# A gated recurrence and its feed-forward layer: the last stores behind the branch, the verdict in the fifth block, a unit between a block's first pieces

## The chip, the cores and the metric

One core of one Trainium2 chip runs the kernel. The metric is the device time of one execution in microseconds (us). The kernel before takes 513.67 us, the median of 3 runs (513.63 to 514.79). TensorE is called PE here, VectorE DVE, ScalarE ACT, GpSimd POOL and SyncE SP; SP issues most of the DMAs.

## The reference

The input of the feed-forward layer is the output of a gated recurrence over 768 steps, 4 batches, 8 heads and 48 channels:

```python
f = 1.0 / (1.0 + np.exp(-f_logit))
for t in range(S):                                   # S = 768
    state = f[:, :, t, :, None] * state + np.einsum('bhd,bhe->bhde', k[:, :, t], v[:, :, t])
    y[:, :, t] = np.einsum('bhd,bhde->bhe', q[:, :, t], state)
x = y.transpose(0, 2, 1, 3).reshape(B * S, H * D)    # 3072 x 384
h = x @ w_in                                         # 384 -> 2048
r = np.maximum(h, 0.0)
return (r * r) @ w_out                               # 2048 -> 384
```

All of it is float32.

## The kernel before

*Blocks and pieces.* The 768 steps are cut into 6 blocks (`NBLK`) of 128 steps; with 4 batches a block has 512 columns. The feed-forward layer of a block is 16 pieces `f` (`NF`) of 128 hidden channels. Each float32 operand is held as a high and a low part, and a product is three matmuls. For each piece `up(f)` is nine matmuls of 128x512 into one hidden bank of PSUM (`ph`, line 246); `square(f)` is three ACT instructions (relu L256, square L257, cast to `gh` L258); `rest(f)` is one DVE instruction (`gl`, L263), the last reader of the bank; `down(f)` is nine matmuls (L272) into the three output banks `po`. `run` issues `up(n)`, `square(n)`, `rest(n)` and then `down(n - 2)` (`LAG`). So at a block's start up(0), up(1) and up(2) follow each other on PE with no down between them, and later up and down alternate. There are two hidden banks, `ps_h0` and `ps_h1`, which take turns (`bank`).

*Order.* Block 0's first 6 pieces are issued from a table written by hand, together with the decoding of the first weights. Then `order` runs block 1 whole, the other 10 pieces of block 0, and blocks 2 to 5 whole. PE, DVE, ACT and SP keep program order.

*Units.* The recurrence is split into units, four per block (three of their own loads and a fourth put together from what the three leave over). A unit's stages, by their letters: L and v loads (DMAs on SP), G gates (ACT), K keys (DVE, POOL), Q queries (DVE), m a copy of the last keys and queries (DMA on SP), T four transposes into the PSUM tile `pk` (PE, L460), N copies out of it (`kn`, ACT, L466), D state sums and S scores, both into `ds` (PE, L484 and L495), r, M, C the crossed rows, the mask and the chain of states (ACT, DVE), s a copy of the states (`sx`, ACT, L454), Y outputs into `py` (PE, L538 and L550), H, X, g and h parts that write the next block's `x`. `hook(k, n, place, do)` puts a stage at run k behind or ahead of piece n: place 0 is ahead of `up(n)`, 0.5 behind `square(n)`, 0.7 behind `rest(n)`, 1 behind `down(n - 2)`. A tuple (n, place, stages) in `STAGE_AT` is relative to the unit's own piece, which is in `UNIT_AT` (`THIRD_AT` for block 2, which is built during blocks 1 and 0); `OUT_AT` is the piece of the outputs. During block b the units of block b + 1 are built. All of a unit's PSUM tiles (`pk`, `ds`, `py` and the like) come from the pool `ps_a`.

*Decoding.* The weights come in as packed words; the 20 halves that remain for block 0's second part are decoded during block 1 on ACT (L139, cast L171) and DVE (L153 to L160, L173), some three halves per two pieces.

*The end.* `finish` copies the three output banks of the last block on ACT, DVE and ACT and issues its stores on SP. Then a verdict is found: the least value in `low` and a test of `sums` (DVE, L853 to L861) go through a PE transpose (`pl`, L863) into a `flag`, all engines read it (`values_load`, L868), and the branch `tc.If(rv > 0)` (L869) leads around a general path, which handles inputs that the fast path cannot. It isn't entered with these inputs. L928 is the closing of the program.

Of the kernel before, what the change touches and what calls it, by code (L numbers as in the profile page):

```python
# [12 lines left out]
F32 = mybir.dt.float32  # L13
# [65 lines left out]
class Moe:  # L79


    def __init__(self, ctx, tc, const, sums, out):
        self.tc, self.nc, self.sums, self.out = tc, tc.nc, sums, out

        self.const, self.raw, self.w, self.ps, self.turns = const, {}, {}, {}, 0
        self.xs, self.spares, self.w4 = [], 0, None

        self.floor = const.tile([P, 1], F32, name="floor")
        tc.nc.vector.memset(self.floor, -31.0 / 64.0)
# [135 lines left out]
        ]  # L225

    def bank(self, f):
        self.ph[f] = self.ps["ps_h1" if self.turns % 2 else "ps_h0"].tile(
            [P, 512], F32, tag="ph", name=f"ph{self.blk}_{f}"
        )  # L230
        self.turns += 1

    def up(self, f, last=True):
# [30 lines left out]
            out=gl, in0=self.ph.pop(f), in1=gh.bitcast(F32), op=ALU.subtract  # L264
        )

    def down(self, f):
        gh, gl = self.g.pop(f)
        for e in range(NJ):
            wh, wl = (self.w[f, 1][:, i, e * P : (e + 1) * P] for i in range(2))  # L270
            for i, (l, r) in enumerate(((wh, gl), (wl, gh), (wh, gh))):
                self.nc.tensor.matmul(  # L272
                    self.po[e], lhsT=l, rhs=r, start=f == self.fs[0] and i == 0,
                    stop=f == self.fs[-1] and i == 2,
                )
# [49 lines left out]
def fast_path(ctx, tc, moe, ident, low, fkqT, vN, w, w4, out):  # L325
    nc = tc.nc
# [344 lines left out]
    with tc.manual_schedule(engines={ET.PE, ET.SP, ET.DVE, ET.Activation}):  # L671
        with tc.tile_pool(name="ps_p", bufs=2, space=bass.MemoryType.PSUM) as ps_p:
            for t in FIRST.split():
                step(t)
        moe.psum(ctx, "ps_h1", "ps_o")

        moe.sums_of()
        for t in SECOND.split():
            step(t)
        part = moe.keep()  # L680
        whole = half[0] + half[1]
        order = [(1, whole), (0, half[1])] + [(blk, whole) for blk in range(2, NBLK)]
# [14 lines left out]
        halves = [(f, i) for f in half[1] for i in range(2)]  # L697
        steps = [moe.decode(f, i, pro, False) for f, i in halves]
        for n in range(NF - 1):
            few = range(3 * n // 2, min(3 * (n + 1) // 2, len(halves)))  # L700
            for h in few:
                if n < AHEAD:
                    weights_load(*halves[h])
                else:
                    hook(0, n - AHEAD, 0.5, lambda h=h: weights_load(*halves[h], mark=True))

            def before(few=few):
                for h, last in zip(few, (None, *few)):
# [12 lines left out]

            hook(0, n, 0, before)
            hook(0, n, 0.5, after)
            hook(0, n, 0.7, last)
        hook(0, NF - 1, 0, third)
        for blk in range(2, NBLK):
            first = 0 if blk == 2 else (blk - 1) * NF - LO
            ats = (THIRD_AT, THIRD_OUT_AT) if blk == 2 else (UNIT_AT, OUT_AT)
            for j, (at, out_at) in enumerate(zip(*ats)):
                un = Unit(blk * HP + j, xs, (ps_a,))  # L730
                for n, place, stage in STAGE_AT if un.own else LAST_AT:
                    hook(0, first + at + n, place, lambda un=un, stage=stage: un.stage(stage))
                out_stage = "YHX" if un.own else "YHXhg"
                hook(0, first + out_at, 1, lambda un=un, stage=out_stage: un.stage(stage))
        for k, (blk, fs) in enumerate(order):
            if blk > 1 and blk + 1 < NBLK:
                xs[blk + 1] = moe.new_x(blk + 1, (0, 1, 2)[blk - 2])
            moe.start(blk, xs[blk], fs)
            moe.run(hooks[k])
            moe.finish(lambda e: out[blk, e * P : (e + 1) * P], None if blk else part)  # L740


def general_path(ctx, tc, moe, ident, fkqT, vN, w, out):

    nc = tc.nc
    dram = ctx.enter_context(tc.tile_pool(name="dram", bufs=1, space=bass.MemoryType.DRAM))
    xs = dram.tile([HP, D, 2, B, S], F32, name="xs")
    with ExitStack() as att:
        pool = att.enter_context(tc.tile_pool(name="gen", bufs=1))
# [6 lines left out]
        for hp in range(HP):  # L756
# [16 lines left out]
            ff = src["f"]  # L773
# [67 lines left out]
@with_exitstack  # L841
def tile_kernel(ctx: ExitStack, tc: tile.TileContext, fkqT, vN, w, w4, out):
    nc = tc.nc
    const = ctx.enter_context(tc.tile_pool(name="const", bufs=1))
    ident = const.tile([P, P], F32, name="ident")
    low = const.tile([P, NBLK * NJ, B * NC], F32, name="low")
    sums = const.tile([P, 2 * NF], F32, name="sums")
    moe = Moe(ctx, tc, const, sums, out)
    with ExitStack() as fast:
        fast_path(fast, tc, moe, ident, low, fkqT, vN, w, w4, out)  # L850


    flag = const.tile([1, 1], I32, name="flag")  # L853
    with tc.tile_pool(name="ps_l", bufs=1, space=bass.MemoryType.PSUM) as ps_l:
        good = const.tile([P, 2], F32, name="good")
        nc.vector.tensor_reduce(
            out=good[:, 0:1], in_=low.rearrange("p u n -> p (u n)"), axis=mybir.AxisListType.X, op=ALU.min
        )
        nc.vector.tensor_scalar(out=sums, in0=sums, scalar1=MOST, scalar2=None, op0=ALU.is_lt)
        nc.vector.tensor_reduce(out=good[:, 1:2], in_=sums, axis=mybir.AxisListType.X, op=ALU.min)  # L860
        nc.vector.tensor_tensor(out=good[:, 0:1], in0=good[:, 0:1], in1=good[:, 1:2], op=ALU.min)  # L861
        pl = ps_l.tile([1, P], F32, name="pl")
        nc.tensor.transpose(out=pl, in_=good[:, 0:1], identity=ident)  # L863
        least = const.tile([1, 1], F32, name="least")
        nc.vector.tensor_reduce(out=least, in_=pl, axis=mybir.AxisListType.X, op=ALU.min)
        nc.vector.tensor_scalar(out=least, in0=least, scalar1=LOWEST, scalar2=None, op0=ALU.is_le)
        nc.vector.tensor_copy(out=flag, in_=least)
    rv = nc.values_load(flag[0:1, 0:1], min_val=0, max_val=1)  # L868
    with tc.If(rv > 0):  # L869
# [63 lines left out]
```

## Time and profile before

| | |
|---|---|
| median of 3 runs | 513.67 us (513.63 to 514.79) |
| the profiled execution | 515.19 us, its span 513.4 us |
| TensorE clock granted, mean | 0.996 |
| PE busy | 490.2 us, 95% of the span |
| PEld (weight loads) busy | 390.0 us, 76% |
| ACT busy | 285.1 us, 56% |
| DVE busy | 261.4 us, 51% |
| POOL busy | 29.2 us, 6% |

A profile's page shows one execution. Its span runs from the first to the last recorded instruction. In the rows of the timeline the columns are the start, the duration, the engine, the line of the kernel, the operation, output and inputs, a shape and a count; brackets at the end give the idle time just before and whose work ended it. In the rows by line, the part ahead of the bar names the operation, its shape and count; behind it stand the busy time in us and the mean in ns of one instruction, then the idle time before it. The waits are sum, count and median. SPq, DVEq and ACTq are the sequencers of these engines; their rows of a line give the minimum, median and maximum duration in ns and the first and last time of it.

### The profile page before, as it was taken

The page shows a single profiled execution, that of the slowest core. Times are in us where ns is not written, and L with a number is a line of the kernel's source. Part 1 is how long each engine was busy: PE and PEld are TensorE (multiplying, and loading weights), DVE is VectorE, ACT ScalarE, POOL GpSimd, SP SyncE. Part 2 cuts the span into 40 slices and gives each one's busy share as a digit, 9 for nine tenths or more (in the row PEclk, how much of TensorE's full clock was granted, in tenths as well). Part 3 has the DMA queues.
Part 4 walks back from the last instruction along what each step waited for, and adds up shares of the span by engine and source line. Part 5 has one row for each costly group of instructions (what it writes and reads, how often), then busy time and mean ns, then how long its engine had stood idle before and what let it go on. Part 6 is the DMA issues. An engine that isn't in the chain of part 4 may idle for free.

```text
span 513.4 us, 11450 instructions
## 1 busy us (share of the span) xinstructions
PE 490.2 (95%) x4831; PEld 390.0 (76%) x4831; DVE 261.4 (51%) x479; ACT 285.1 (56%) x579; POOL 29.2 (6%) x66
## 2 busy tenths in 40 slices
PE   6689899999999999999999999999999999999994
PEld 5577676888777778778787787787777787788883
DVE  7899977988847263554353445353346222211111
ACT  4689748877756563554544555454555543544441
POOL 6112010001000000000000000000000000000000
PEclk9999999999999999999999999999999999999998
DMA  8982026473332116203005313004410001100001
GB/s 284 312 301 68 13 69 244 133 250 107 88 90 48 42 22 172 77 15 88 3 5 145 109 28 89 1 1 119 139 28 12 1 1 32 62 1 1 0 1 68
DMA packets 20364, 41.97 MB, mean 82 GB/s; under 512 B 2656, under 2 KB 5728, under 8 KB 20304
## 3 DMA queue, kind: packets, MB, share of 16 engines
q1 hardware_dynamic: 19856, 40.23, 25.9%
q0 software_dynamic: 448, 0.92, 0.8%
q8 instruction: 40, 0.66, 0.5%
q14 instruction: 20, 0.16, 0.1%
HBM read 31.69 MB, written 4.72 MB: 71 GB/s over the span
## 4 chain that ended last, share of the span: by engine, by line
PE 82%; DVE 9%; ACT 3%; DMA 3%; issue 1%; SPq 0%; POOL 0%; DVEq 0%; ACTq 0%
PE po L272 37%; PE ph L246 35%; PE ds L495 2%; PE ds L484 2%; PE py L538 2%; DMA last_kq<-fkq 2%; PE py L550 2%; DVE fkq L410 1%; PE pk L460 1%; DMA fkq<-in_fkqT_dram 1%; DVE gl L263 1%; DVE fkq L424 1%; ACT gh L258 1%; ACT ph L257 1%; ACT ph L256 1%
## 5 line engine op out<-in xcount | busy, mean ns | idle before, releaser
L246 PE MATMUL ph<-x,w 128*128 128x512 f32 x864 | 221.8, 402 | 3.1 <-DVE gl L263 3.1
L246 PEld LDWEIGHTS ph<-x,w 128*128 128x128 f32 x864 | 159.8, 189 | 43.2 <-DVE gl L263 5.8
L272 PE MATMUL po<-gh,w 128*128 128x512 f32 x576 | 181.0, 395 | 0.3 <-DVE w L173 0.3
L263 DVE TENSOR_TENSOR gl<-ph,gh 128x512 fp32r<-128x512 f32 x96 | 66.2, 690 | 186.7 <-ACT gh L258 186.6
L256 ACT ACTIVATE ph<-ph 128x512 f32<-128x512 f32 x96 | 55.9, 582 | 142.2 <-PE ph L246 142.2
L272 PEld LDWEIGHTS po<-gh,w 128*128 128x128 f32 x576 | 107.9, 187 | 26.8 <-DVE w L173 0.6
L272 PE MATMUL po<-gl,w 128*128 128x512 f32 x288 | 114.1, 396 | 0.0
L272 PEld LDWEIGHTS po<-gl,w 128*128 128x128 f32 x288 | 54.0, 187 | 13.3 <-issue 0.2
L258 ACT CAST gh<-ph 128x512 fp32r<-128x512 f32 x96 | 56.3, 586 | 3.0
L257 ACT ACTIVATE ph<-ph 128x512 f32<-128x512 f32 x96 | 55.9, 582 | 3.0
L415 POOL TENSOR_SCALAR fkq<-fkq 128x8 f32<-128x8 f32 x18 | 11.8, 657 | 326.1 <-DVE fkq L410 308.6
L410 DVE TENSOR_TENSOR_SCAN fkq<-fz,dr 128x520 f32<-128x520 f32 x18 | 22.2, 1235 | 4.8 <-ACT fz L405 4.8
L538 PEld LDWEIGHTS py<-sc,vn 64*64 64x64 f32 (+1 forms) x640 | 17.9, 126 | 8.1 <-issue 7.0
L171 ACT CAST w<-wa 128x384 fp32r<-128x384 f32 (+1 forms) x33 | 16.8, 510 | 12.4 <-DVE wa L160 10.5
L424 DVE TENSOR_TENSOR_SCAN fkq<-fz,dz 128x520 f32<-128x520 f32 x18 | 22.3, 1241 | 0.6
L538 PE MATMUL py<-sc,vn 64*64 64x64 f32 (+1 forms) x640 | 21.1, 222 | 0.7 <-DVE sc L502 0.7
L502 DVE TENSOR_TENSOR sc<-ds,mask 128x512 f32<-128x512 f32 x24 | 16.5, 689 | 10.2 <-PE ds L495 9.6
L139 ACT ACTIVATE wa<-raw 128x384 f32<-128x384 f32 (+1 forms) x33 | 18.1, 550 | 5.1 <-DMA raw<-in_w_dram 5.0
L550 PE MATMUL py<-rx,sx 48*48 48x64 f32 (+1 forms) x320 | 20.3, 217 | 0.1
L460 PE MATMUL pk<-ident,fkq 128*128 128x128 f32 x72 | 13.6, 318 | 5.3 <-DVE fkq L416 3.4
L156 DVE SCALAR_TENSOR_TENSOR wa<-raw,wa 128x384 int32<-128x384 int32 (+1 forms) x33 | 18.1, 552 | 0.8
L454 ACT COPY sx<-sp 48x208 f32<-48x208 f32 x44 | 16.0, 365 | 3.9 <-DVE sp L517 2.9
(92 smaller groups left out, 408.2 us busy)
## 6 DMA issues: line engine op xcount, KB each, us to landing
fkq<-in_fkqT_dram SPq DMA_DIRECT2D x17, 768.0 KB, 5.6
raw<-in_w_dram SPq DMA_DIRECT2D x32, 384.0 KB, 5.3
vn<-in_vN_dram SPq DMA_DIRECT2D x24, 192.0 KB, 5.1
out_dram<-ob SPq DMA_DIRECT2D x15, 256.0 KB, 2.3
x<-ys SPq DMA_DIRECT2D x30, 64.0 KB, 2.4
last_kq<-fkq SPq DMA_DIRECT2D x28, 64.5 KB, 2.3
out_dram<-part SPq DMA_DIRECT2D x3, 256.0 KB, 2.1
last_kq<-fkq POOLq DMA_DIRECT2D x8, 64.5 KB, 5.8
```

The costliest lines, as they stand in the source:

```text
L139: nc.scalar.activation(a, upper_f, AF.Abs, scale=2.0**-112, **kw)
L246: self.nc.tensor.matmul(self.ph[f], lhsT=w[:, i], rhs=x[:, j], start=first and n == 0, stop=last and n == 2)
L256: nc.scalar.activation(ph, ph, AF.Relu)
L257: nc.scalar.activation(ph, ph, AF.Square)
L258: nc.scalar.copy(out=gh, in_=ph)
L263: self.nc.vector.tensor_tensor(out=gl, in0=self.ph.pop(f), in1=gh.bitcast(F32), op=ALU.subtract)
L272: self.nc.tensor.matmul(self.po[e], lhsT=l, rhs=r, start=f == self.fs[0] and i == 0, stop=f == self.fs[-1] and i == 2,)
L410: V.tensor_tensor_scan(out=rr[:, ::-1], data0=self.fz[:, NZ * CZ : 0 : -1], data1=dr[:, ::-1], initial=0.0, op0=ALU.mult, op1=ALU.add,)
L424: V.tensor_tensor_scan(out=pp, data0=self.fz[:, : NZ * CZ], data1=dz, initial=0.0, op0=ALU.mult, op1=ALU.add)
L460: nc.tensor.transpose(out=self.pk[:, b], in_=self.kt[:, b * TB : (b + 1) * TB], identity=ident)
L538: nc.tensor.matmul(self.py[h * C : h * C + m, c, b * C : (b + 1) * C], lhsT=self.vn[rows, b, h * D : h * D + m], rhs=self.sc[rows, h, b], ...
L550: nc.tensor.matmul(self.py[h * C : h * C + m, c, b * C : (b + 1) * C], lhsT=s[rows, b * D : b * D + m], rhs=q[rows], start=False, stop=b = ...
```

## The change

Five things are changed.

1. One unit per block gets stages of its own, `EARLY_AT`: its transposes stand behind up(0) of the run (`UNIT_AT` 0 in place of −3), its state sums behind up(1). That is unit 0 of blocks 3, 4 and 5; of block 2, which is built around block 0's second part, it is unit 1, with its own piece at 16 in place of 15.
2. The decoding of the remaining weights stands one piece later in block 1; the first part stands whole behind `rest(1)`.
3. The verdict is found in block 4 (the fifth), behind `down(10)` of piece 12, and read by the engines in block 5 behind piece 12. Its transpose uses the tile `pk` of `ps_a`; the pool of its own is gone.
4. In block 5, for which no unit is built any more, the hidden banks rotate over three: `ps_h0`, `ps_h1` and `pk`. Its last two downs are interleaved by output bank, and all three copies are DVE's.
5. The last block's stores stand behind the branch in SP's program. The general path now writes its outputs of the last block and loads them back into the copied tiles first.

The diff, without the lines that only move the verdict's instructions:

```diff
+EARLY_AT = ((-4, 0, "Lv"), (-2, 1, "GK"), (-1, 0.5, "Q"), (-1, 1, "m"), (0, 1, "TN"), (1, 1, "DSrMC"), (2, 1, "s"))
-UNIT_AT, OUT_AT = (-3, 3, 6, 9), (3, 6, 9, 13)
-THIRD_AT, THIRD_OUT_AT = (11, 15, 18, 21), (15, 18, 21, 23)
+UNIT_AT, OUT_AT = (0, 3, 6, 9), (3, 6, 9, 13)
+THIRD_AT, THIRD_OUT_AT = (11, 16, 18, 21), (15, 18, 21, 23)
+EARLY, THIRD_EARLY = 0, 1
+VERDICT_AT = 12
...
     def bank(self, f):
+        n = self.turns % (3 if self.third_bank else 2)
+        pool, tag = (self.ps[f"ps_h{n}"], "ph") if n < 2 else (self.third_bank, "pk")
+        self.ph[f] = pool.tile([P, 512], F32, tag=tag, name=f"ph{self.blk}_{f}")
...
-    def run(self, hooks):
+    def run(self, hooks, obs=None):
         for n in range(len(self.fs) + LAG):
+            if obs and n == len(self.fs):
+                for e in range(NJ):
+                    for f in self.fs[-LAG:]:
+                        self.down(f, (e,))
+                    self.nc.vector.tensor_copy(out=obs[e], in_=self.po[e])
+                return
...
-        for n in range(NF - 1):
-            few = range(3 * n // 2, min(3 * (n + 1) // 2, len(halves)))
+        for n in range(1, NF - 1):
+            few = range(3 * (n - 1) // 2, min(3 * n // 2, len(halves)))
...
-            hook(0, n, 0, before)
-            hook(0, n, 0.5, after)
-            hook(0, n, 0.7, last)
+            for place, do in zip((0, 0.5, 0.7) if n > 1 else (0.7, 0.7, 0.7), (before, after, last)):
+                hook(0, n, place, do)
...
-                for n, place, stage in STAGE_AT if un.own else LAST_AT:
+                for n, place, stage in EARLY_AT if j == early_unit else STAGE_AT if un.own else LAST_AT:
...
+        hook(len(order) - 2, VERDICT_AT, 1, lambda: general.append(verdict(nc, moe, low, ident, ps_a)))
+        hook(
+            len(order) - 1, VERDICT_AT, 1,
+            lambda: general.append(nc.values_load(general[0][0:1, 0:1], min_val=0, max_val=1)),
+        )
...
-            moe.run(hooks[k])
-            moe.finish(lambda e: out[blk, e * P : (e + 1) * P], None if blk else part)
+            if blk == NBLK - 1:
+                moe.third_bank = ps_a
+                obs = [moe.gp.tile([P, NT], F32, tag=f"part{e}", name=f"ob_last{e}", bufs=1) for e in range(NJ)]
+                moe.run(hooks[k], obs)
+                moe.third_bank = None
+            else:
+                moe.run(hooks[k])
+                moe.finish(lambda e: out[blk, e * P : (e + 1) * P], None if blk else part)
+    return general[1], obs
...
     with tc.If(rv > 0):
         with ExitStack() as gen:
             general_path(gen, tc, moe, ident, fkqT, vN, w, out)
+        for e in range(NJ):
+            nc.sync.dma_start(obs[e], out[NBLK - 1, e * P : (e + 1) * P])
+    for e in range(NJ):
+        nc.sync.dma_start(out[NBLK - 1, e * P : (e + 1) * P], obs[e])
```

In the rows that follow the numbers after a name are block, then unit or piece, then a running number; the lines of the changed kernel stand some lines lower (up is L251 there, down L277, the transposes L472, the state sums L496, the scores L507, the verdict's transpose L781, the branch L899).

PE at the start of block 3, before; `w15_1` is the last down of block 2, `w0_0` the first up of block 3:

```order
L272 MATMUL po2_0_2_2544<-gh2_15_3301,w15_1_1791 128x512 x2
L246 MATMUL ph3_0_3351<-x3_0_2539,w0_0_524 128x512 x3
L246 MATMUL ph3_0_3351<-x3_1_2540,w0_0_524 128x512 x3
L246 MATMUL ph3_0_3351<-x3_2_2541,w0_0_524 128x512 x3
L246 MATMUL ph3_1_3367<-x3_0_2539,w1_0_486 128x512 x3
L246 MATMUL ph3_1_3367<-x3_1_2540,w1_0_486 128x512 x3
L246 MATMUL ph3_1_3367<-x3_2_2541,w1_0_486 128x512 x3
L246 MATMUL ph3_2_3387<-x3_0_2539,w2_0_731 128x512 x3
```

The same place of PE after, where `pk4_0` and `ds4_0` belong to unit 0 of block 4:

```order
L277 MATMUL po2_0_2_2494<-gh2_15_3248,w15_1_1824 128x512 x2
L251 MATMUL ph3_0_3301<-x3_0_2489,w0_0_524 128x512 x3
L251 MATMUL ph3_0_3301<-x3_1_2490,w0_0_524 128x512 x3
L251 MATMUL ph3_0_3301<-x3_2_2491,w0_0_524 128x512 x3
L472 MATMUL pk4_0_3317<-ident_58,fkq4_0_3108 128x128 x4
L251 MATMUL ph3_1_3325<-x3_0_2489,w1_0_486 128x512 x3
L251 MATMUL ph3_1_3325<-x3_1_2490,w1_0_486 128x512 x3
L251 MATMUL ph3_1_3325<-x3_2_2491,w1_0_486 128x512 x3
L496 MATMUL ds4_0_3341<-vn4_0_3110,kn4_0_3322 64x48
...
L507 MATMUL ds4_0_3341<-fkq4_0_3108 64x64 x16
L251 MATMUL ph3_2_3387<-x3_0_2489,w2_0_731 128x512 x3
```

The transposes moved in between up(0) and up(1), the state sums and scores (32 small matmuls, most of them in the rows left out) between up(1) and up(2); before, they stood in block 2's pieces 13 and 14.

DVE at piece 12 of block 4, after; before, the `gl` of pieces 12 and 13 were neighbours:

```order
L268 TENSOR_TENSOR gl4_12_4731<-ph4_12_4720,gh4_12_4730 128x512
L774 TENSOR_REDUCE good_4746<-low_59 128x1
L777 TENSOR_SCALAR sums_60<-sums_60 128x32
L778 TENSOR_REDUCE good_4746<-sums_60 128x1
L779 TENSOR_TENSOR good_4746<-good_4746 128x1
L783 TENSOR_REDUCE least_4753<-pl_4751 1x1
L784 TENSOR_SCALAR least_4753<-least_4753 1x1
L785 CAST flag_4745<-least_4753 1x1
L268 TENSOR_TENSOR gl4_13_4768<-ph4_13_4757,gh4_13_4767 128x512
```

Between these two `gl` the verdict's seven instructions now stand; the fifth of them waits for PE's transpose. On PE after, at the same place:

```order
L277 MATMUL po4_0_2_4106<-gl4_10_4637,w10_1_1487 128x512
L277 MATMUL po4_0_2_4106<-gh4_10_4636,w10_1_1487 128x512 x2
L781 MATMUL pl_4751<-ident_58,good_4746 1x128
L251 MATMUL ph4_13_4757<-x4_0_3295,w13_0_1614 128x512 x3
L251 MATMUL ph4_13_4757<-x4_1_3296,w13_0_1614 128x512 x3
```

The transpose of `good` moved in between down(10) and up(13). SP's end before:

```order
L868 TENSOR_LOAD flag_5310
L868 ISA x2
L314 DMA out_0_dram<-ob4_0_4878 128x512
L314 DMA out_0_dram<-ob4_1_4881 128x512
L314 DMA out_0_dram<-ob4_2_4884 128x512
L314 DMA out_0_dram<-ob5_0_5290 128x512
L314 DMA out_0_dram<-ob5_1_5293 128x512
L314 DMA out_0_dram<-ob5_2_5296 128x512
L869 COMPARE_AND_BRANCH
```

and after, where the rows left out are those of the general path:

```order
L326 DMA out_0_dram<-ob4_2_4898 128x512
L752 TENSOR_LOAD flag_4745
L752 ISA x2
L899 COMPARE_AND_BRANCH
...
L899 UNCONDITIONAL_BRANCH x2
L906 DMA out_0_dram<-ob_last0_4904 128x512
L906 DMA out_0_dram<-ob_last1_4905 128x512
L906 DMA out_0_dram<-ob_last2_4906 128x512
L963 UNCONDITIONAL_BRANCH
```

SP's read of the flag and its branch moved ahead of the last block's three stores, which now stand behind the general path.

More of the change, by code (lines that the diff above doesn't have):

```diff
@@ L85, in __init__ @@
         self.const, self.raw, self.w, self.ps, self.turns = const, {}, {}, {}, 0
-        self.xs, self.spares, self.w4 = [], 0, None
+        self.xs, self.spares, self.w4, self.third_bank = [], 0, None, None
         self.floor = const.tile([P, 1], F32, name="floor")
@@ L227, in bank @@
     def bank(self, f):
-        self.ph[f] = self.ps["ps_h1" if self.turns % 2 else "ps_h0"].tile(
-            [P, 512], F32, tag="ph", name=f"ph{self.blk}_{f}"
-        )
+        n = self.turns % (3 if self.third_bank else 2)
+        pool, tag = (self.ps[f"ps_h{n}"], "ph") if n < 2 else (self.third_bank, "pk")
+        self.ph[f] = pool.tile([P, 512], F32, tag=tag, name=f"ph{self.blk}_{f}")
         self.turns += 1
@@ L265, in rest, with down @@
         )
-    def down(self, f):
-        gh, gl = self.g.pop(f)
-        for e in range(NJ):
+    def down(self, f, es=range(NJ)):
+        gh, gl = self.g[f]
+        for e in es:
             wh, wl = (self.w[f, 1][:, i, e * P : (e + 1) * P] for i in range(2))
@@ L606, in fast_path @@
     moe.inputs(ctx)
-    moe.hidden(ctx)
     ps_a = ctx.enter_context(tc.tile_pool(name="ps_a", bufs=1, space=bass.MemoryType.PSUM))
@@ L728, in fast_path @@
             ats = (THIRD_AT, THIRD_OUT_AT) if blk == 2 else (UNIT_AT, OUT_AT)
+            early_unit = THIRD_EARLY if blk == 2 else EARLY
             for j, (at, out_at) in enumerate(zip(*ats)):
                 un = Unit(blk * HP + j, xs, (ps_a,))
-                for n, place, stage in STAGE_AT if un.own else LAST_AT:
+                for n, place, stage in EARLY_AT if j == early_unit else STAGE_AT if un.own else LAST_AT:
                     hook(0, first + at + n, place, lambda un=un, stage=stage: un.stage(stage))
@@ L734, in fast_path @@
                 hook(0, first + out_at, 1, lambda un=un, stage=out_stage: un.stage(stage))
+        general = []
+        hook(len(order) - 2, VERDICT_AT, 1, lambda: general.append(verdict(nc, moe, low, ident, ps_a)))
[3 more added lines that the diff above has]
+        )
         for k, (blk, fs) in enumerate(order):
@@ L738, in fast_path, with verdict @@
             moe.start(blk, xs[blk], fs)
-            moe.run(hooks[k])
-            moe.finish(lambda e: out[blk, e * P : (e + 1) * P], None if blk else part)
+            if blk == NBLK - 1:
[7 more added lines that the diff above has]
+    return general[1], obs
+def verdict(nc, moe, low, ident, pool):
+    flag = moe.const.tile([1, 1], I32, name="flag")
+    good = moe.const.tile([P, 2], F32, name="good")
+    nc.vector.tensor_reduce(
+        out=good[:, 0:1], in_=low.rearrange("p u n -> p (u n)"), axis=mybir.AxisListType.X, op=ALU.min
+    )
+    nc.vector.tensor_scalar(out=moe.sums, in0=moe.sums, scalar1=MOST, scalar2=None, op0=ALU.is_lt)
+    nc.vector.tensor_reduce(out=good[:, 1:2], in_=moe.sums, axis=mybir.AxisListType.X, op=ALU.min)
+    nc.vector.tensor_tensor(out=good[:, 0:1], in0=good[:, 0:1], in1=good[:, 1:2], op=ALU.min)
+    pl = pool.tile([1, P], F32, tag="pk", name="pl")
+    nc.tensor.transpose(out=pl, in_=good[:, 0:1], identity=ident)
+    least = moe.const.tile([1, 1], F32, name="least")
+    nc.vector.tensor_reduce(out=least, in_=pl, axis=mybir.AxisListType.X, op=ALU.min)
+    nc.vector.tensor_scalar(out=least, in0=least, scalar1=LOWEST, scalar2=None, op0=ALU.is_le)
+    nc.vector.tensor_copy(out=flag, in_=least)
+    return flag
 def general_path(ctx, tc, moe, ident, fkqT, vN, w, out):
@@ L816, in general_path @@
         moe.inputs(ff)
-        moe.hidden(ff)
         moe.psum(ff, "ps_h0", "ps_h1", "ps_o")
@@ L848, in tile_kernel @@
     moe = Moe(ctx, tc, const, sums, out)
+    moe.hidden(ctx)
     with ExitStack() as fast:
[L850 to L868, printed above, removed]
+        rv, obs = fast_path(fast, tc, moe, ident, low, fkqT, vN, w, w4, out)
     with tc.If(rv > 0):
```

## The prediction

> **What bounds the kernel now.** I read, in this order, the page (busy rows, the chain of work that ended last), the waits, PE's timeline at every block's start, and the rows of the end.
>
> ```profile
> PE 490.2 (95%) x4831; PEld 390.0 (76%) x4831; DVE 261.4 (51%) x479; ACT 285.1 (56%) x579; POOL 29.2 (6%) x66
> PE 82%; DVE 9%; ACT 3%; DMA 3%; issue 1%; SPq 0%; POOL 0%; DVEq 0%; ACTq 0%
> PE ph L246 <- DVE gl L263: 3.1, 6, 0.5
> ```
>
> The first row gives each engine's busy time, the second the chain's shares, the third a wait: PE's up matmuls (L246) waited 3.1 us in six places for the DVE instruction that frees the hidden bank (L263). So PE sets the pace nearly throughout: only its stops, its extra matmuls and the time after its last matmul can move the end. One of the six stops, at block 3's start:
>
> ```profile
> 280.90 4.36 PE L246 MATMUL ph<-x,w 128*128 128x512 f32 x18
> 284.43 0.59 ACT L258 CAST gh<-ph 128x512 fp32r<-128x512 f32 x1
> 285.05 0.69 DVE L263 TENSOR_TENSOR gl<-ph,gh 128x512 fp32r<-128x512 f32 x1 [3.95 <-ACT gh L258]
> 285.79 2.36 PE L246 MATMUL ph<-x,w 128*128 128x512 f32 x9 [0.53 <-DVE gl L263]
> 287.99 0.39 PE L272 MATMUL po<-gl,w 128*128 128x512 f32 x1
> ```
>
> A regular piece, in block 4:
>
> ```profile
> 417.89 0.40 PE L272 MATMUL po<-gl,w 128*128 128x512 f32 x1
> 419.99 2.26 PE L246 MATMUL ph<-x,w 128*128 128x512 f32 x9
> ```
>
> That is the cadence: nine matmuls take 2.10 from start to start. Up(0) and up(1) (x18) take 4.20 from 280.90, so up(2) could start at 285.10. It starts at 285.79, when bank 0 has passed ACT and DVE: 0.69 late. Its nine last 2.20 instead of 2.10 (to 287.99), another 0.10. So a stop costs 0.79. Two of the six stand in block 1, one each in the runs after it (second half of block 0, blocks 2 to 5).
>
> **The change part by part.** The profiled execution took 515.19, 1.52 above the median of 513.67, and its span is 513.4; 1.79 lies outside. The sum is of differences inside that span, carried over to the median unchanged.
>
> *(a) A unit's pieces at the starts of blocks 2, 3 and 4.* The four transposes now stand between up(0) and up(1), the state and score matmuls between up(1) and up(2). What they cost where they stand between two nines today:
>
> ```profile
> 124.68 0.60 PE L460 MATMUL pk<-ident,fkq 128*128 128x128 f32 x4
> 125.04 2.35 PE L246 MATMUL ph<-x,w 128*128 128x512 f32 x9
> 127.55 0.54 ACT L466 COPY kn<-pk 128x448 f32<-128x448 f32 x1
> 129.41 0.60 PE L484 MATMUL ds<-vn,kn 64*64 64x48 f32 x29
> 130.50 2.35 PE L246 MATMUL ph<-x,w 128*128 128x512 f32 x9
> ```
>
> 0.36 and 1.09, together 1.45, and about 0.1 for each change of shape. No matmul is added: this work only moves into time in which PE stood. It delays up(2) by 1.45 to 1.65, more than the 0.69 needed, so the stop goes. Of each 0.79 I subtract 0.09, since transposes that shared a gap with other small matmuls now make one of their own: 3 × 0.70 = −2.1. Its cover is kn: the L466 copy follows ACT's L258 (285.02) and would end near 285.5, while the state matmuls want it at 283.0 + 0.36 + 2.2 = 285.6. If it is later, PE waits there instead. Bounds −2.4 (nothing subtracted) to −1.2 (half the gain lost). The unit's other steps move too: its loads (DMAs on SP) come three pieces later than today, still four pieces (16.8 by the cadence) ahead of the transposes; gates on ACT, keys on DVE and their bound on POOL two pieces later, queries and SP's copy of the last keys in the piece before the transposes. None of it is on PE, DVE is 51% busy, and I cost it at nothing; the slack towards the outputs, which stay at piece 3, is used up, so a late state copy would appear as a wait there, as in (f).
>
> *(b) Block 5's third bank.* No unit is left for block 5; up(2) goes into a bank of its own, and so has nothing to wait for: −0.8 (0 if the bank's last reader were late; it is block 4's).
>
> *(c) The end.*
>
> ```profile
> 505.67 0.69 DVE L313 COPY ob<-po 128x512 f32<-128x512 f32 x1 [3.06 <-PE po L272]
> 506.37 0.58 ACT L313 COPY ob<-po 128x512 f32<-128x512 f32 x1 [0.82 <-DVE ob L313]
> DMA to landing us min/median/max: 2.0/3.3/3.8
> L869 DVEq COMPARE_BRANCH  x1: 72/72/72, 506.3 to 506.3; - x1
> L869 DVEq EVENT_SEMAPHORE  x1: 21/21/21, 509.8 to 509.8; - x1
> L869 SPq COMPARE_BRANCH  x1: 45/45/45, 507.4 to 507.4; - x1
> L869 SPq EVENT_SEMAPHORE  x8: 17/17/17, 511.2 to 511.7; - x8
> L928 SPq EVENT_SEMAPHORE  x14: 17/28/28, 511.8 to 513.3; - x14
> ```
>
> The branch (L869) takes 0.07, but the next instruction comes 3.5 later on DVE and 3.8 later on SP. SP branches at 507.4, behind the stores, and goes on at 511.2, then needs 2.2 for its joins to 513.4. After the change SP has branched long before. The last copy, now DVE's, starts at 506.37 and ends at 507.06; the store issues then and lands 2.0 to 3.8 later. DVE's branch row (506.3) precedes its copy's end (506.36), so the jump overlaps the copy: 506.39 + 3.47 = 509.86. That is the later of the two at a landing of 2.0 to 2.7. Behind it I estimate 0.35 for the joins left (some 14 of 0.02 to 0.03) and 0.8 for the closing barrier, part of the 511.8 to 513.3 row: 511.05, so −2.3. Bounds −1.0 (most joins still in line) and −2.8 (barrier alone). The Trainium skill (Runtime: NRT & Kernel Launch, Instruction fetch mechanics) says that a taken branch out of the loaded pages forces a fetch before execution goes on; the 3.5 and 3.8 agree.
>
> *(d) The verdict in block 4.*
>
> ```profile
> 419.94 0.69 DVE L263 TENSOR_TENSOR gl<-ph,gh 128x512 fp32r<-128x512 f32 x1 [3.51 <-ACT gh L258]
> L856 DVE TENSOR_REDUCE good<-low 128x1 f32<-128x144 f32 x1 | 0.3, 302 | 0.1
> L859 DVE TENSOR_SCALAR sums<-sums 128x32 f32<-128x32 f32 x1 | 0.2, 181 | 0.1
> L860 DVE TENSOR_REDUCE good<-sums 128x1 f32<-128x32 f32 x1 | 0.2, 179 | 0.0
> L861 DVE TENSOR_TENSOR good<-good 128x1 f32<-128x1 f32 x1 | 0.1, 132 | 0.0
> 433.88 0.27 PE L863 MATMUL pl<-ident,good 128*1 128x128 f32 x1
> ```
>
> DVE starts gl of piece 12 at 419.94 and ends at 420.63. The four instructions (0.302 + 0.181 + 0.179 + 0.132 = 0.79) make good ready at 421.42. On PE the transpose stands ahead of up(13), which started at 419.99 and would now start behind it, at about 421.45 to 421.5 plus 0.1 for the transpose. PE has nothing it may run meanwhile: +1.57; and I take back 0.11 where the transpose stands today (an estimate: its 0.27 mostly overlaps the matmul behind it) = +1.46. Bounds 1.2 (instructions overlapping) and 1.8 (longer hops). Everything behind up(13) only shifts. Reading the flag in block 5 stands behind gl and gh of piece 12 on DVE and ACT and before up(13) on PE; the flag is some 75 us old then, and I cost it at nothing.
>
> *(e) The weights' decode one piece later (block 1).*
>
> ```profile
> 76.93 4.35 PE L246 MATMUL ph<-x,w 128*128 128x512 f32 x18
> 81.82 2.37 PE L246 MATMUL ph<-x,w 128*128 128x512 f32 x9 [0.54 <-DVE gl L263]
> 83.77 0.51 ACT L171 CAST w<-wa 128x384 fp32r<-128x384 f32 x1 [1.25 <-DVE wa L160]
> 84.19 0.58 ACT L256 ACTIVATE ph<-ph 128x512 f32<-128x512 f32 x1
> 86.03 0.69 DVE L263 TENSOR_TENSOR gl<-ph,gh 128x512 fp32r<-128x512 f32 x1 [0.42 <-ACT gh L258]
> 86.78 2.37 PE L246 MATMUL ph<-x,w 128*128 128x512 f32 x9 [0.49 <-DVE gl L263]
> ```
>
> The first stop (81.82) is untouched. The second (86.78) comes from a decode cast ahead of the relu on ACT. One piece (4.2) later the same chain runs 84.19 + 4.2 = 88.4 to 90.9, and up(4), which without stops would start 4.2 after an unhindered up(3), at 90.2, waits 0.7 to 0.8. The stop moves rather than goes: +0.1, bounds −0.8 (it goes) and +0.6 (two casts in front).
>
> *(f) Block 2's unit 1* now has its last state copied (sx) in the piece in which its outputs need it, as unit 3 does today. First a unit without that, at 158.85:
>
> ```profile
> 158.85 0.34 PE L538 MATMUL py<-sc,vn 64*64 64x64 f32 x8
> 160.07 0.65 PE L460 MATMUL pk<-ident,fkq 128*128 128x128 f32 x4
> ```
>
> and that unit 3:
>
> ```profile
> 185.50 0.34 PE L538 MATMUL py<-sc,vn 64*64 64x64 f32 x8
> 187.10 0.66 PE L460 MATMUL pk<-ident,fkq 128*128 128x128 f32 x4
> ```
>
> Outputs take 1.22 undisturbed (first pair) and 1.60 with that wait (second): +0.4, bounds −0.2 and +0.8.
>
> *(g) The last two downs interleaved:* the first one of piece 15 comes 1.4 earlier, close to its gl: +0.1 (0 to 0.3).
>
> Sum: −2.1 − 0.8 − 2.3 + 1.5 + 0.1 + 0.4 + 0.1 = −3.1. That makes 512.1 of the profiled 515.19, and **510.5** of the median.
>
> **The rivals.**
> - *The verdict costs nothing*, if PE's transpose is not late because DVE gets to gl earlier than I think. Against: DVE starts gl when ACT's cast ends (419.94, 3.51 idle before), 0.05 before up(13). It would give 510.5 − 1.46 = 509.1.
> - *The last store decides.* If it lands 3.75 after its issue (507.09), SP goes on at 510.84 and ends near 512.0: the end gives 1.4, the time is 511.4. For it: the 3.8 maximum above. Against: that transfer met the branch's instruction fetches, which DVE and ACT still make. The Trainium skill (Advanced Engine Details and Errata, Control Flow Timing) gives about 108 ns for a compare-and-branch; by that SP's 3.8 was this landing, and the sum would be 511.4 too; DVE's 3.5 behind no transfer speaks against it.
> - *The stops only move on*, as in (e): ACT gets kn's copy between two squares, so that up(3) of blocks 2 to 4 waits for the bank that up(2) no longer waits for. 3 × 0.70 stays: 512.6, within the bound. Against: down(0) stands between up(2) and up(3), which gives ACT 2.1 more; for it, block 1's second stop has just that form.
> - *Slower: the jumps after the branch are taken.* The changed program ends the untaken path with two further unconditional jumps on every engine. If DVE really fetches anew for each at 3.47 as above, the end moves to 509.86 + 6.94 + 1.15 = 518.0, +4.6 instead of −2.3: 517.4. It decides once one more fetch (3.47) outweighs the rest of the gain. Against: between 509.8 and 511.7 in the rows above no second gap of that size stands, though today's program has a jump there too.
>
> **How the numbers follow.** The forecast has 0.60; verdict hidden (509.1) 0.10; landing (511.4) 0.12; stops move on (512.6) 0.11; jumps 0.05; the rest 0.02. What a measurement of this kernel can tell from no change is 0.3%, 1.54 us: faster is below 512.13. The forecast's own bounds, not all added, give 509.4 to 511.8. The range reaches over the three rivals of the same sign, with as much again for their terms: 509.0 to 512.8, leaving out the jumps and the tails. Faster: 0.60 + 0.10 + 0.12 less a tail, 0.82; same: 0.11 and a tail, 0.13; slower 0.05.
>
> **What would show it.** (a) No wait of up(2) in blocks 2 to 4, transposes directly behind up(0), and no longer wait of the state matmuls for kn. (b) 27 up matmuls of block 5 in one row. (c) SP's branch near 445, a last store at about 504, and an end that follows DVE's branch by some 4.7; a store that lands last means the second rival. (d) PE idle for some 1.4 ahead of up(13) of block 4. (e) One stop at up(2) and one at up(4) of block 1. The forecast is wrong most likely through (c), whose terms behind the jump are estimates, or if new waits come with the units, which have less slack than today.

## The result, and the profile after

The changed kernel takes 511.31 us, the median of 7 runs (509.76 to 512.96), the kernel before 514.27 in 7 runs of the same sessions (513.63 to 515.44): ratio 0.9946, 95% interval 0.9925 to 0.9968. That is 2.96 us less, by the interval 1.6 to 3.9; 3.1 less was forecast. The profiled execution took 511.15, its span is 509.4.

The page's busy row, the shares of the chain, and three of PE's waits for DVE (sum, count, longest: the third figure of a wait is its longest, not the median that the part on the profile before names):

```profile
PE 490.5 (96%) x4831; PEld 391.3 (77%) x4831; DVE 263.0 (52%) x483; ACT 284.0 (56%) x577; POOL 29.2 (6%) x66
PE 78%; DVE 12%; ACT 4%; DMA 3%; issue 2%; POOL 0%; SPq 0%; DVEq 0%; ACTq 0%; POOLq 0%
PE ph L251 <- DVE gl L268: 0.7, 1, 0.7
PE pl L781 <- DVE good L779: 1.2, 1, 1.2
PE po L277 <- DVE gl L268: 0.4, 1, 0.4
```

PE does the same work (490.5 for 490.2). Of 3.1 us in six waits of ups for gl, 0.7 is left here (and one row of 0.5 at block 1's first stop, put down to another DVE instruction). Two waits are new: 1.2 for the verdict's `good`, 0.4 of a down for its gl.

The executions differ early: block 0's first up starts between 33.4 and 36.3 us, and block 1 between 74.9 and 77.6, in the thirteen traces of this study, whichever kernel. So traces are compared from block 1's first up, by the starts of PE's matmuls. Runs that share a stretch agree in it within 0.1, but for block 1's first six pieces in one run, named below. PE's end is the end of its last matmul, and the end is that of the span:

| stretch, start to start | before | after | difference |
|---|---|---|---|
| up(0) of block 1 to its up(6) | 22.56 | 22.70 | +0.14 |
| up(15) of block 1 to up(9) of block 0 | 21.48 | 22.53 | +1.05 |
| up(13) of a run to up(2) of block 2 / 3 / 4 | 25.26 / 24.66 / 24.66 | 24.50 / 23.87 / 23.87 | −2.34 |
| up(12) of block 4 to up(0) of block 5 | 22.39 | 23.78 | +1.39 |
| up(0) to up(3) of block 5 | 9.19 | 8.39 | −0.80 |
| up(15) of block 5 to PE's end | 8.57 | 8.65 | +0.08 |
| the rest, up to PE's end | 270.64 | 270.36 | −0.28 |
| block 1 to PE's end | 429.41 | 428.65 | −0.76 |
| PE's end to the end | 7.06 | 4.64 | −2.42 |

The two profiled spans differ by 4.0; the 0.78 that isn't in the table is the earlier start. So most of the gain is in the end. On PE, 3.1 gained at the starts of blocks 2 to 5 is given back but for 0.8. The start of block 3, to be held against the rows at 280.90 to 287.99 of before:

```profile
278.75 2.26 PE L251 MATMUL ph<-x,w 128*128 128x512 f32 x9
280.84 0.60 PE L472 MATMUL pk<-ident,fkq 128*128 128x128 f32 x4
281.19 2.34 PE L251 MATMUL ph<-x,w 128*128 128x512 f32 x9
282.75 0.54 ACT L478 COPY kn<-pk 128x448 f32<-128x448 f32 x1
283.46 0.60 PE L496 MATMUL ds<-vn,kn 64*64 64x48 f32 x29
284.56 2.36 PE L251 MATMUL ph<-x,w 128*128 128x512 f32 x9
```

Transposes, up(1), state sums and up(2) follow each other without a wait. kn ends at 283.29, 0.17 ahead of the matmul that reads it.

The verdict in block 4, PE and DVE in order of time:

```profile
413.74 2.26 PE L251 MATMUL ph<-x,w 128*128 128x512 f32 x9
417.88 0.69 DVE L268 TENSOR_TENSOR gl<-ph,gh 128x512 fp32r<-128x512 f32 x1 [3.50 <-ACT gh L263]
418.49 0.29 DVE L774 TENSOR_REDUCE good<-low 128x1 f32<-128x144 f32 x1
419.12 0.16 DVE L779 TENSOR_TENSOR good<-good 128x1 f32<-128x1 f32 x1
419.34 0.27 PE L781 MATMUL pl<-ident,good 128*1 128x128 f32 x1 [1.25 <-DVE good L779]
419.36 2.35 PE L251 MATMUL ph<-x,w 128*128 128x512 f32 x9
```

Up(12) to up(13) takes 5.62 in place of 4.20. The kernel before has the verdict's instructions behind the last block in its text, but its profile has them earlier than that: `good` was ready at 390.3, in block 4, and its transpose ran at 433.88, between two downs (the prediction shows that row).

```profile
L861 DVE TENSOR_TENSOR good<-good x1: 132/132/132, 390.2 to 390.2; 128x1 f32<-128x1 f32 x1
```

So the change doesn't bring the verdict from the end into block 4. It moves `good`, which was ready some 43 us ahead of its transpose, to right in front of it. And block 1, whose stops are at up(2) and now at up(4):

```profile
81.03 2.37 PE L251 MATMUL ph<-x,w 128*128 128x512 f32 x9 [0.53 <-DVE raw L376]
85.33 2.26 PE L251 MATMUL ph<-x,w 128*128 128x512 f32 x9
90.36 2.37 PE L251 MATMUL ph<-x,w 128*128 128x512 f32 x9 [0.68 <-DVE gl L268]
```

The end: the branch's rows on SP and DVE, the last copy, and SP's last waits in the order of their lengths:

```profile
504.83 0.69 DVE L289 COPY ob_last<-po 128x512 f32<-128x512 f32 x1 [0.71 <-PE po L277]
L899 SPq COMPARE_BRANCH  x1: 45/45/45, 439.7 to 439.7; - x1
L899 DVEq COMPARE_BRANCH  x1: 72/72/72, 504.9 to 504.9; - x1
L899 DVEq EVENT_SEMAPHORE  x1: 21/21/21, 507.8 to 507.8; - x1
SPq L963 <- DVEq L899: 1.4, 1, 1.4
SPq L963 <- PEq L963: 0.7, 2, 0.5
SPq L963 <- DMA out_dram<-ob_last: 0.5, 1, 0.5
```

SP branches at 439.7. DVE goes on at 507.8, about 3.0 after its branch. Then SP still waits 0.5 for the last store's landing (0.7 belongs to the closing barrier). While SP jumps (439.7 to 442.3), the DMA view of that stretch has one transfer of instructions (count, MB, share of the DMA engines' time):

```profile
q14 instruction: 1, 0.01, 1.3%
```

### The profile page after: what moved, and what is told of

Its sections match the earlier page's. It is cut to its first block, busy times and chain, and to the rows that moved or that the text cites. A ratio compares the mean times of both kernels' runs of the same rounds, so it can differ in the third digit from the quotient of the medians.

```text
span 509.4 us, 11456 instructions
## 1 busy us (share of the span) xinstructions
PE 490.5 (96%) x4831; PEld 391.3 (77%) x4831; DVE 263.0 (52%) x483; ACT 284.0 (56%) x577; POOL 29.2 (6%) x66
## 4 chain that ended last, share of the span: by engine, by line
PE 78%; DVE 12%; ACT 4%; DMA 3%; issue 2%; POOL 0%; SPq 0%; DVEq 0%; ACTq 0%; POOLq 0%
PE ph L251 36%; PE po L277 33%; PE ds L507 2%; PE ds L496 2%; PE py L550 2%; PE py L562 2%; DVE fkq L436 1%; DMA last_kq<-fkq 1%; DVE gl L268 1%; DVE fkq L422 1%; DMA fkq<-in_fkqT_dram 1%; DVE wa L161 1%; PE pk L472 1%; ACT ph L262 1%; DVE w L178 1%
## 5 line engine op out<-in xcount | busy, mean ns | idle before, releaser
L251 PE MATMUL ph<-x,w 128*128 128x512 f32 x864 | 222.4, 402 | 1.2 <-DVE gl L268 0.7
L251 PEld LDWEIGHTS ph<-x,w 128*128 128x128 f32 x864 | 160.0, 189 | 39.2 <-DVE gl L268 1.1
L277 PE MATMUL po<-gh,w 128*128 128x512 f32 x576 | 180.4, 394 | 0.3 <-DVE w L178 0.3
L277 PEld LDWEIGHTS po<-gh,w 128*128 128x128 f32 x576 | 108.1, 188 | 26.6 <-DVE w L178 0.6
L277 PE MATMUL po<-gl,w 128*128 128x512 f32 x288 | 114.7, 398 | 0.4 <-DVE gl L268 0.4
L277 PEld LDWEIGHTS po<-gl,w 128*128 128x128 f32 x288 | 54.1, 188 | 13.7 <-DVE gl L268 1.1
L422 DVE TENSOR_TENSOR_SCAN fkq<-fz,dr 128x520 f32<-128x520 f32 x18 | 22.3, 1237 | 6.7 <-ACT fz L417 6.6
L562 PEld LDWEIGHTS py<-rx,sx 48*48 48x48 f32 (+1 forms) x320 | 18.1, 127 | 0.5 <-ACT sx L466 0.5
L178 DVE TENSOR_TENSOR w<-wa,w 128x384 fp32r<-128x384 f32 (+1 forms) x33 | 18.0, 546 | 0.7 <-ACT w L176 0.6
```

The lines of the kernel that those rows point to most:

```text
L178: nc.vector.tensor_tensor(out=w[:, 1], in0=a, in1=w[:, 0].bitcast(F32), op=ALU.subtract)
L251: self.nc.tensor.matmul(self.ph[f], lhsT=w[:, i], rhs=x[:, j], start=first and n == 0, stop=last and n == 2)
L277: self.nc.tensor.matmul(self.po[e], lhsT=l, rhs=r, start=f == self.fs[0] and i == 0, stop=f == self.fs[-1] and i == 2,)
L422: V.tensor_tensor_scan(out=rr[:, ::-1], data0=self.fz[:, NZ * CZ : 0 : -1], data1=dr[:, ::-1], initial=0.0, op0=ALU.mult, op1=ALU.add,)
L562: nc.tensor.matmul(self.py[h * C : h * C + m, c, b * C : (b + 1) * C], lhsT=s[rows, b * D : b * D + m], rhs=q[rows], start=False, stop=b = ...
```

## The experiments

All of them are read by the stretches of the table above; one execution of each was profiled, and where no median is given, it is the only one.

**The verdict in two parts.** DVE's four instructions stay; the transpose and what follows stand one piece later.

```diff
+        hook(len(order) - 2, VERDICT_AT + 1, 1, lambda: general.append(verdict_end(nc, moe, general.pop(), ident, ps_a)))
...
```

> The verdict's four DVE instructions stay behind gl of piece 12 of block 4; its PE transpose and what follows it stand one piece later. Theory: the 1.25 us stop ahead of up(13) is PE waiting for good and nothing else, so up(12) to up(13) falls from 5.62 to 4.2, the transpose costs about 0.1 where it now stands, and the span behind block 1 is shorter by 1.3. Rival: the four instructions also make the next gl late, so that the stop reappears as a wait of a down for gl, and the span behind block 1 stays within 0.3 of what it is.

```profile
417.63 2.26 PE L251 MATMUL ph<-x,w 128*128 128x512 f32 x9
418.83 0.16 DVE L779 TENSOR_TENSOR good<-good 128x1 f32<-128x1 f32 x1
423.00 0.27 PE L787 MATMUL pl<-ident,good 128*1 128x128 f32 x1
423.03 1.17 PE L251 MATMUL ph<-x,w 128*128 128x512 f32 x4
```

`good` is ready 4 us ahead of its transpose, and the next up starts 0.03 behind the transpose. Up(12) to up(15) takes 13.86 in place of 15.39, with nothing given back: −1.44 at the stop and −0.10 in the two pieces behind it. The theory holds. The kernel before takes 13.89 there.

**The decode back.** Only the shift of block 1's decode is undone.

```diff
-        for n in range(1, NF - 1):
-            few = range(3 * (n - 1) // 2, min(3 * n // 2, len(halves)))
+        for n in range(NF - 1):
+            few = range(3 * n // 2, min(3 * (n + 1) // 2, len(halves)))
...
```

> Only the decode's shift is undone (it starts at piece 0 of block 1 again). Theory: the 0.39 us wait of block 1's down(15) for gl, which cost 0.65 in start to start, comes from the decode's DVE work, which pushed block 2's unit 1's keys and queries 1.5 us later and with them gl of piece 15. It goes (-0.65), and the second stop of block 1 goes back from up(4) to up(3) and is 0.16 cheaper: -0.8 in all up to block 0's second part. Rival: the wait comes from the unit's later place; then it stays, and the difference is -0.16 or less.

Up(15) of block 1 to up(9) of block 0 takes 21.90 in place of 22.53 (−0.63), up(2) to up(6) of block 1 17.64 for 17.81 (−0.17): −0.8 as expected, and the down waits no more. The wait, in the changed kernel, whose up(15) starts at 138.27:

```profile
141.45 1.23 DVE L422 TENSOR_TENSOR_SCAN fkq<-fz,dr 128x520 f32<-128x520 f32 x1
145.06 0.69 DVE L439 TENSOR_TENSOR fkq<-fkq 128x512 f32<-128x512 f32 x1
145.66 0.68 DVE L268 TENSOR_TENSOR gl<-ph,gh 128x512 fp32r<-128x512 f32 x1
146.40 0.50 PE L277 MATMUL po<-gl,w 128*128 128x512 f32 x1 [0.39 <-DVE gl L268]
```

With the decode back, where up(15) starts at 136.87:

```profile
137.72 1.23 DVE L422 TENSOR_TENSOR_SCAN fkq<-fz,dr 128x520 f32<-128x520 f32 x1
```

In both, gl of piece 15 stands behind the unit's keys (L422) and queries on DVE. With the shifted decode ahead of them they start 3.2 us behind up(15) in place of 0.9, so gl ends later and PE's down waits.

**Block 2's unit 1 back.**

```diff
-THIRD_AT, THIRD_OUT_AT = (11, 16, 18, 21), (15, 18, 21, 23)
-EARLY, THIRD_EARLY = 0, 1
+THIRD_AT, THIRD_OUT_AT = (11, 15, 18, 21), (15, 18, 21, 23)
+EARLY, THIRD_EARLY = 0, -1
```

> Only block 2's unit 1 goes back to its old place (piece 15, old stages), the decode stays shifted. Theory: its transposes now need queries that end on DVE near 145.7, while PE would want them near 143.6; PE waits some 2 us there, the 0.65 wait of down(15) and the 0.4 for the copied states go, and the 0.75 stop at block 2's start comes back: slower by 1 to 1.8 up to up(2) of block 2. Rival: moves are independent, the unit's place alone cost 1.05 and saved 0.75, so 0.3 faster.

Both were wrong: up(15) of block 1 to up(9) takes 21.76 in place of 22.53, 0.77 less, and block 2's start is unchanged at 24.50. (This is the one run whose first six pieces of block 1 differ: 22.91 for 22.70, by a longer up(0) and up(1); I have no cause for it.) The transposes read keys, which were ready, not queries:

```profile
143.67 0.66 PE L472 MATMUL pk<-ident,fkq 128*128 128x128 f32 x4
146.46 0.50 PE L277 MATMUL po<-gl,w 128*128 128x512 f32 x1
```

They run while the down would wait for gl anyway, so in the old place they cost nothing as long as the decode is shifted. And what I had priced as the stop that this unit's move fills, block 2's, is filled by unit 0 of block 3; this unit's move, into block 0's second part, fills none. It only costs: 0.5 for the states copied in the piece of the outputs (with the restart), and 0.3 for transposes and state sums in gaps of their own. The decode's 0.63 and the unit's 0.77 share a part: with both back (below, "Both together") the stretch takes 21.46, which is 1.07 less and not 1.40.

**Unit 0 of blocks 3 to 5 back.**

```diff
-UNIT_AT, OUT_AT = (0, 3, 6, 9), (3, 6, 9, 13)
-EARLY, THIRD_EARLY = 0, 1
+UNIT_AT, OUT_AT = (-3, 3, 6, 9), (3, 6, 9, 13)
+EARLY, THIRD_EARLY = -1, 1
```

> Unit 0 of blocks 3 to 5 goes back to its old place and stages; the rest of the change stays. Theory: the stops of up(2) in blocks 2, 3 and 4 return with 0.53 idle each, and from up(13) of one run to up(2) of the next takes 0.75 to 0.80 longer, 2.35 in all. Rival (stops only move): the stops were gone for another reason, or others go at the same time; then it is less than 1.5 slower.

The three stretches take 25.27, 24.64 and 24.64: +2.31. The stop is back, at block 3:

```profile
285.92 2.37 PE L251 MATMUL ph<-x,w 128*128 128x512 f32 x9 [0.53 <-DVE gl L268]
```

**Block 5 with two banks** (the assignment of its third one left out).

> Block 5 goes back to two hidden banks. Theory: up(2) of block 5 waits 0.53 again and up(1) to up(3) takes 6.99 in place of 6.30 less 0.01, 0.80 longer with the restart; nothing else moves. Rival: the stop was hidden by something else, 0.3 or less.

Up(0) to up(3) takes 9.19 in place of 8.39: 0.80.

**The stores ahead of the branch.**

```diff
+    for e in range(NJ):
+        nc.sync.dma_start(out[NBLK - 1, e * P : (e + 1) * P], obs[e])
     with tc.If(rv > 0):
...
-    for e in range(NJ):
-        nc.sync.dma_start(out[NBLK - 1, e * P : (e + 1) * P], obs[e])
```

> The last three stores go back ahead of the branch in SP's order, and the reload in the general path goes; the rest of the change stays. Theory: SP's branch stands behind the last store again (about 1 us after PE's last matmul), its jump of 3.8 starts only then, and from PE's last matmul to the end takes 6.8 to 7.1, as in the kernel before, in place of 4.6 to 5.0; everything up to PE's end stays. Rival: the early verdict or the copies on DVE made the gain, then 4.6 to 5.5.

PE's end to the end takes 6.24, between the two ranges. SP waits in the branch again, though not as long as before:

```profile
L901 SPq COMPARE_BRANCH  x1: 45/45/45, 507.3 to 507.3; - x1
L901 SPq EVENT_SEMAPHORE  x8: 17/17/17, 510.2 to 510.7; - x8
SPq L901 <- SPq L901: 2.8, 1, 2.8
```

2.8, where the kernel before shows 3.8. Over the seven traces with the changed end, all three stores and all copies on DVE, PE's end to the end takes 4.62 to 5.20 (median 4.77); over the three with the old end, 6.79 to 7.06. So the place of the stores is worth about 1.5 of the 2.3, by one trace, and the rest goes with a shorter jump. In this kernel ACT branches at 501.0, 6 us ahead of SP; in the kernel before DVE, ACT and SP jumped between 506.3 and 507.4. That jumps at the same time make each other longer would fit, and wasn't tried by itself. Against the plain form of it: with the last copy on ACT (below), ACT's jump (500.6 to 503.1) overlaps DVE's (499.2 to 502.3) and is no longer than the 2.4 to 2.7 that ACT's takes in the other traces made from the changed kernel.

**Two stores in place of three.** The last store is left out, so a third of the last block's output is not written.

```diff
-    for e in range(NJ):
+    for e in range(NJ - 1):
         nc.sync.dma_start(out[NBLK - 1, e * P : (e + 1) * P], obs[e])
```

> The last of the last block's three stores is left out (a sixth of the output's last... one third of the last block's output is not written). Theory: after the change the end waits for this store's landing, about 0.5 behind DVE's join of the branch, so from PE's last matmul to the end goes from 4.64 to 4.1. Rival, the prediction's own step: DVE's jump behind the branch decides, and the 4.64 stays within 0.15.

```profile
SPq L963 <- DVEq L899: 2.9, 1, 2.9
SPq L963 <- PEq L963: 0.7, 2, 0.5
```

4.23: 0.4 less than the changed kernel's execution, and SP's wait for a landing is gone. With all stores the landing comes last, by about half a microsecond; without the last one DVE's jump does. The seven traces say the same: the last store lands 2.9 to 3.5 us after its issue, and the later it lands, the later the end comes, from 4.62 to 5.20 behind PE's end.

**Another way to take the stops away.** In the kernel before, piece 2 of blocks 1 to 5 (in block 1 also 5 and 8) goes into `pk`, and nothing is moved.

```diff
...
     def bank(self, f):
+        if self.third_bank and f in self.third_at:
+            self.ph[f] = self.third_bank.tile([P, 512], F32, tag="pk", name=f"ph{self.blk}_{f}")
+            return
...
+            moe.third_bank, moe.third_at = ps_a, {1: (2, 5, 8), 2: (2,), 3: (2,), 4: (2,), 5: (2,)}.get(blk, ())
             moe.run(hooks[k])
+            moe.third_bank = None
```

> The kernel before, with piece 2 of blocks 1 to 5 (and 5 and 8 of block 1) in the unit's bank pk and no other change: no unit, verdict or store is moved. Theory: a stop at a block's start is nothing but the missing third bank, so all six go: 4 x 0.79 in blocks 2 to 5 and 0.79 + 0.76 in block 1, 4.7 shorter between block 1 and PE's last matmul. Rival: in block 1 ACT and DVE are late with the decode, so that the second stop comes back as a wait of a down for gl, and the units' transposes wait for the bank: 3.2 to 3.9 shorter.

Block 1 to PE's end takes 424.71 in place of 429.41: 4.70 less. At block 3 three ups stand in one row:

```profile
278.15 6.46 PE L249 MATMUL ph<-x,w 128*128 128x512 f32 x27
```

From up(13) to up(3) over the starts of blocks 2 to 4 this kernel takes 85.09, the changed kernel 85.14 and the kernel before 87.46: at these three stops the idle bank and the moved units are worth the same. The bank also takes away both stops of block 1 (up(0) to up(6) 21.00 for 22.56) and that of block 5, and costs nothing elsewhere. The one run took 509.73, less than the changed kernel's median, with the old end.

**Both together.** Verdict in two parts, decode and all units in their old places, `pk` for the pieces named above (every third in block 5), the stores behind the branch.

> The changed kernel with its verdict in two parts, units and decode in their old places, and the bank pk for piece 2 of blocks 1 to 5 (2, 5, 8 in block 1; every third in block 5). Theory: against the changed kernel -1.5 (verdict), -1.05 (block 2's unit), -0.15 (decode), -1.5 (both stops of block 1), 0 at the starts of blocks 2 to 4: -4.2, near 507.1 us. Rival: block 1's stops come back as waits for gl, and pk is late for the units: -2.7, near 508.6.

507.49 us, the median of 5 runs (505.51 to 507.69); ratio to the kernel before 0.9869, interval 0.9849 to 0.9890. Block 1 to PE's end takes 424.20, 4.45 less than in the changed kernel; no wait of an up or a down is left behind block 1's start.

**The last copy on ACT**, added to that one.

```diff
-                    self.nc.vector.tensor_copy(out=obs[e], in_=self.po[e])
+                    (self.nc.scalar.copy if e == NJ - 1 else self.nc.vector.tensor_copy)(out=obs[e], in_=self.po[e])
```

> The fastest version so far, with the last of the three copies on ACT in place of DVE. Theory (the last store's landing decides the end): the copy is 0.1 shorter, 0.58 in place of 0.69, so the end comes 0.1 earlier, too little to be measured. Rival (DVE's jump decides): DVE branches 1.4 earlier and ACT's jump is the late one, 0.5 or more earlier.

508.19 (506.59 to 508.96), ratio 0.9880, interval 0.9858 to 0.9901: not to be told from the one before. The shift shows in SP's waits:

```profile
SPq L971 <- DMA out_dram<-ob_last: 2.6, 2, 2.0
SPq L971 <- DVEq L907: 0.2, 1, 0.2
```

DVE's join is 1.2 earlier and only lengthens the wait for the landing. The landing decides. It took 3.8 here and 3.5 in the run before, so PE's end to the end is 5.41 for 5.20: the 0.1 gained at the copy doesn't show.

**The pool of the hidden pieces alone**, in the kernel before:

```diff
-    moe.hidden(ctx)
...
-        moe.hidden(ff)
...
+    moe.hidden(ctx)
     with ExitStack() as fast:
```

> The kernel before, with only the pool of the hidden pieces (gh, gl) opened ahead of the fast path, as the change does; no instruction moves. Theory: this placing of the tiles makes an up and a down of nine 4.187 in place of 4.20 each (block 1's pieces 6 to 15 39.43 in place of 39.51, block 5's 3 to 15 50.24 in place of 50.40), and nothing else. Rival: the pace depends on something else of the changed program, and stays 39.51 and 50.40.

39.47 and 50.32, halfway between the two kernels (39.51 and 50.40; 39.43 and 50.24). So neither is shown. The granted clock isn't the cause: 50.24 stands in traces with a mean clock of 0.977 (the verdict in two parts) and of 0.999 (the changed kernel).

## Why the prediction was right

The time came out mostly by the forecast mechanisms. In two places it was luck: at the end two wrong steps cancel, and on PE a cost priced 0.65 too low, (f), is offset by a gain priced 0.24 too low, (a), and by a faster pace that wasn't forecast.

- *(a) Units at the starts of blocks 2 to 4:* −2.34 for −2.1. I had subtracted 0.09 for each block, as a price of gaps of their own; bringing the old places back cost 2.31, so it wasn't there. The cover held: kn was ready 0.17 ahead.
- *(b) Third bank:* −0.80, as forecast; shown by taking it away.
- *(c) The end:* −2.42 in the profiled execution, −2.3 by the median of seven, for −2.3. The step was only half right: by the prediction's own sign, a store that lands last, the path is the second rival's. DVE's jump took 3.0 and not 3.47, and the last store, which had to land within 2.0 to 2.7 for DVE to be last, landed 2.9 after its issue, 0.5 after DVE's join, a price of 0.5 and not the rival's 0.9. That the two errors cancel is luck. (The sum for the end is 511.01, where the prediction has 511.05.) The Trainium skill (Runtime: NRT & Kernel Launch, Instruction fetch mechanics) has a taken branch wait for a fetch of its target when that isn't loaded; the trace agrees, with a transfer of instructions during SP's jump, as shown above. The jumps of SP, ACT and DVE here took 2.4 (ACT, in the rows of the changed kernel, 499.7 to 502.1) to 3.0, against branch rows of 0.05 to 0.07:

```profile
L899 ACTq COMPARE_BRANCH  x1: 50/50/50, 499.7 to 499.7; - x1
L899 ACTq EVENT_SEMAPHORE  x1: 17/17/17, 502.1 to 502.1; - x1
```

- *(d) The verdict:* +1.39 for +1.46, and the split shows that it is a wait of PE alone. The price was avoidable: the kernel before paid only for the transpose itself, about 0.1. The first rival falls.
- *(e) The decode:* +0.14 for +0.1; the stop moved from up(3) to up(4). What the sum missed is that the same shift is felt at the other end of block 1: DVE's later decode makes gl of piece 15 late, 0.65 with the unit in its new place. I had only looked at the stop.
- *(f) Block 2's unit 1:* +1.05 with that wait, for +0.4. The wait for copied states has the forecast size, 1.59 from outputs to transposes for 1.22:

```profile
158.80 0.34 PE L550 MATMUL py<-sc,vn 64*64 64x64 f32 x8
160.39 0.66 PE L472 MATMUL pk<-ident,fkq 128*128 128x128 f32 x4
```

The term was mis-sized because I priced the outputs (0.5) and not the transposes and state sums that got gaps of their own (0.3), nor the down that they had covered (0.65, less the 0.4 that the transposes took in their old place). The list of the six stops in the prediction is wrong too: the rows have two in block 1 and one each in blocks 2 to 5, none in block 0's second part, into which this unit moved.
- *(g)* +0.08 for +0.1.
- *The third rival* (stops only move on) falls at blocks 2 to 5 and is what happened in block 1. *The slower rival* falls: ACT and DVE have one long gap each behind their branch, and none at the two further unconditional jumps.

On PE the terms made −0.8 by the forecast and −0.76 by the trace, though here −0.28 stands in the rest of the table, which the forecast didn't have: −0.25 of it is the faster pace of the last section, in block 1's pieces 6 to 15 and block 5's 3 to 15 (I find none in blocks 2 to 4). Without it PE would have gained 0.5. The end carries what remains. The median came to 511.31 and not 510.5, in part because the kernel before took 514.27 in these sessions and not 513.67.

## What to carry to other kernels

A stop for want of a buffer can be taken away with work moved into it or with a buffer that happens to be idle at that moment. At the same three stops both were worth the same here (2.3 and 2.4 us). The idle bank also reached the two stops of block 1 and, as in the change, that of block 5, 4.7 in all, and it moves nothing; the later decode and the move of block 2's unit 1 lost 1.2 in blocks 1 and 0, where they filled no stop. Before an instruction is put in front of PE in program order, ask when its operand is ready, and stand it one piece behind that. A block of code that isn't entered still costs a jump over it, so let the engine that issues the last stores pass the branch before them; that was worth about 1.5 us here. For the other engines it made no difference that these runs show: DVE's earlier branch gained nothing, because the last landing decides.

## What the runs showed of the hardware

- A jump over the general path took 2.4 to 4.0 us on ACT, DVE and SP, and a transfer of instructions stands in it. In the three traces with the old end it took 3.4 to 4.0, in the ten others 2.4 to 3.1; the cause of the difference is open. PE's branch row itself lasts 3.3 to 3.8. On POOL the next row comes 0.5 after the branch in all thirteen traces.
- A wait of 0.39 or 0.53 of idle on PE costs 0.65 and 0.79 from start to start, so 0.26 beside what the profile books as idle.
- Nine 128x512 matmuls take 2.093 on average in block 5 of the changed kernel and of all made from it, with two banks or three, and 2.100 in the kernel before (50.24 and 50.40 from up(3) to up(15), 24 such groups). With one pool opened earlier they take 2.097; the cause is open.
